# Router and output gates of a fused attention and mixture-of-experts kernel, moved from the vector engine to GpSimd under a new order of work

## The chip, the cores and the metric

The kernel runs on one core of one Trainium2 chip. The metric is device time in microseconds (us), the median of several runs. A run's time contains the span that the profile shows, from the first to the last instruction, and some microseconds around it. The engines are called by their names in the profile: PE multiplies matrices, PEld loads its weights, DVE is the vector engine, ACT the scalar engine, POOL is GpSimd, and SP only issues DMAs.

## The reference, cut to what matters

Two layers stand one after the other: attention over pooled keys and values for 8 heads, whose output is the input x of four causal attention experts, of which each token uses two.

```python
# q, k, v: (8 batches, 8 heads, 576 tokens, 64)
k_p = k.reshape(B, H, Sp, 8, D).mean(axis=3)          # 72 pooled keys
v_p = v.reshape(B, H, Sp, 8, D).mean(axis=3)
attn = softmax(scale * q @ k_p^T); x = (attn @ v_p)   # -> (8, 576, 512)

logits = x @ w_gate                                   # 4 experts
topk = the 2 largest; w = softmax over those two
for e in range(4):
    q, k, v = x @ wq[e], x @ wk[e], x @ wv[e]         # 512 -> 64
    a = softmax(causal(scale * q @ k^T))
    ye = a @ v @ wo[e]                                # 64 -> 512
    out += (e in topk) * w_e * ye
```

## The kernel before

The batches are worked on one after another, with two or three of them in flight at once. There are no loops over the work: line 551 begins a string, SEQ, of 1129 tokens, and lines 642 to 677 read it and issue each token's instructions. The order of the tokens is the order on PE, ACT, DVE and POOL; each engine takes its own tokens strictly in this order and waits for semaphores where data is not there. A token such as `P_q1:5@0c` names the step (P), its argument (q, pair of experts 1), the batch (5), the PSUM bank (0), and has a trailing d if a copy runs on DVE instead of ACT, or c if a matmul is cut into four strips of 32 columns of the PE array.

Capital letters are PE's steps. PK and PV pool keys and values (96x32 tiles of the array); KT, Q and T are transposes; E makes the first attention's scores and S the experts' scores (both use 64 rows of the array); D and O make the denominators and outputs of the first attention (96x32 tiles); P and V project to the experts' queries, keys and values (V also gives the router's logits, four columns wide); B multiplies with the values; Y is the output projection; H is a number of warm-up matmuls that compute nothing. The small letters read PSUM: kc, kt, vc, r, p, v, t and y copy results out (line 176, on ACT or DVE), e and s are exponentials on ACT (lines 267, 273, 427, 433), d and x make reciprocals by logarithm and exponential on ACT (lines 294, 298), o multiplies on DVE (lines 310, 317).

The steps that the change moves are these. `gate` (line 336), tokens g0 to g9 of each batch, turns logits L into weights G: g0 is an exponential on ACT (line 350), g1 to g4 find the second largest logit with pairs of maxima and minima and make a mask (lines 354, 359, 363, 367), g5 multiplies (371), g6 and g7 sum (373, 377), g8 takes a reciprocal (382), g9 multiplies (384). All but g0 are on DVE. `bv` (line 476) has three steps for each part of the experts' output: bz takes a reciprocal of the denominators from PSUM (482), bg multiplies it with G (484), b multiplies the output with that (489). All three are on DVE.

POOL issues every load (tokens L, line 117; L_q2:4 is the third sixth of the queries of batch 4; and W, line 130, for weights). A batch has 6 loads for q, 3 for k, 3 for v. POOL also zeroes the causal blocks after an exponential (token a, `am`, lines 442 and 450). Raw inputs have three buffers each, so a load of batch b waits until batch b-3 has been read. SP issues the output DMAs (lines 540 and 544); the token z, and the output's second half, go to ACT's queue.

Of the kernel before, what the change touches and what calls it, by code (L numbers as in the profile page):

```python
# [12 lines left out]
MINOP = mybir.AluOpType.min  # L13
MAXOP = mybir.AluOpType.max
ISGE = mybir.AluOpType.is_ge
ISLE = mybir.AluOpType.is_le
# [5 lines left out]
def kernel(  # L22
# [12 lines left out]
    nc = tc.nc  # L35
# [3 lines left out]
    E = moe_wq.shape[0]  # L39
# [296 lines left out]
    def gate(b, step):  # L336
# [10 lines left out]
        L = got("L")  # L347
# [3 lines left out]
        elif step == 1:  # L351
            L2 = L.rearrange("p c (a b) -> p c a b", b=2)
            for nm, op in (("hi", MAXOP), ("lo", MINOP)):
                nc.vector.tensor_tensor(
                    out=tmp(nm, 2, 1), in0=L2[:, :, :, 0:1], in1=L2[:, :, :, 1:2], op=op
                )
        elif step == 2:
            for nm, src, op in (("s2", "hi", MINOP), ("s3", "lo", MAXOP)):
                nc.vector.tensor_tensor(
                    out=tmp(nm, 1), in0=got(src)[:, :, 0, :], in1=got(src)[:, :, 1, :], op=op  # L360
                )
        elif step == 3:
            nc.vector.tensor_tensor(
                out=tmp("m2", 1), in0=got("s2"), in1=got("s3"), op=MAXOP
            )
        elif step == 4:
            nc.vector.tensor_tensor(
                out=tmp("msk", E), in0=L, in1=got("m2").to_broadcast([128, n, E]), op=ISGE
            )
        elif step == 5:  # L370
            nc.vector.tensor_mul(out=tmp("W", E), in0=got("Ex"), in1=got("msk"))
        elif step == 6:
            nc.vector.tensor_add(
                out=tmp("d2", 2), in0=got("W")[:, :, 0:2], in1=got("W")[:, :, 2:4]
            )
        elif step == 7:
            nc.vector.scalar_tensor_tensor(
                out=tmp("den", 1), in0=got("d2")[:, :, 0:1], scalar=1e-9,
                in1=got("d2")[:, :, 1:2], op0=ADD, op1=ADD,
            )  # L380
        elif step == 8:
            nc.vector.reciprocal(out=tmp("rden", 1), in_=got("den"))
        else:
            nc.vector.tensor_mul(
                out=tmp("G", E), in0=got("W"), in1=got("rden").to_broadcast([128, n, E])
            )
# [89 lines left out]
    def bv(b, bank, step, ep, part):  # L476
# [6 lines left out]
        elif step == "bg":  # L483
            nc.vector.tensor_mul(
# [26 lines left out]
    def Y(b, bank, c):  # L511
        p0 = 128 * place(b, c)
        last = (b, c) == (B - 1, 4)
        for n0 in (0, 256) if last else (0,):
            n = 256 if last else 512
            for ep in range(NEP):
                wide(psum[:, bank ^ (n0 > 0), n0 : n0 + n],
# [3 lines left out]
    def y(b, bank, dve, c, half=None, later=False):  # L521
        ofin = at[b, "ofin", c] if (b, "ofin", c) in at else ofp.tile([128, DM], FP32, name="ofin", tag="ofin")
        if half is not None:
            cols = slice(256 * half, 256 * half + 256)
            copy(half == 1, ofin[:, cols], psum[:, bank ^ half, cols])
# [10 lines left out]
    def z(b, c, queue):  # L536
# [15 lines left out]
        I:0 L_k0:0 L_k1:0 L_k2:0 J:0 K:0 H19:0@0 PK:0@0 kc:0 H4:0@1 KT:0@0 kt:0 L_q0:0 L_q1:0  # L552
        L_q2:0 L_q3:0 L_q4:0 L_q5:0 H8:0@1 Q2:0@0 r2:0 Q1:0@1 Q3:0@2 r1:0d r3:0 H1:0@3 E2:0@4
        e2:0 Q0:0@1 r0:0 E3:0@2 H5:0@0 E0:0@4 e3:0 L_v0:0 L_v1:0 E4:0@0 L_v2:0 PV:0@6 vc:0d e4:0
        e0:0 H2:0@2 D2:0@0 E1:0@2 O11:0@1 e1:0 H4:0@6 O01:0@2 O20:0@3 D1:0@4 d1:0 D0:0@5 x1:0
        M:0 L_k0:1 L_k1:1 L_k2:1 O10:0@6 O00:0@7 PK:1@4 d0:0 L_q0:1 o10:0 L_q1:1 L_q2:1 L_q3:1
        L_q4:1 kc:1d H3:0@5 KT:1@6 L_q5:1 H5:0@4 Q0:1@4 Q3:1@5 d2:0 x0:0 o01:0 o00:0 kt:1 o11:0
        x2:0 r0:1d W0:0 Q1:1@2 o20:0 W1:0 Q2:1@1 c0:0 E0:1@6 r3:1 r1:1d E3:1@4 c1:0d E1:1@2 e0:1
        c2:0d c3:0d P_q0:0@0 e3:1 W2:0 r2:1d W3:0 e1:1 P_t0:0@6 p_q0:0d p_t0:0d L_v0:1 P_k0:0@1
        S03:0@4 E4:1@6 E2:1@2 P_k1:0@0c c4:0d s03:0 L_v1:1 e4:1 V3:0@4c D2:1@5 D0:1@6 p_k1:0d  # L560
        p_k0:0d v3:0d P_q1:0@7c e2:1 D1:1@0 S00:0@2 d0:1 L_v2:1 d2:1 V1:0@6c p_q1:0d x0:1 s00:0
        V0:0@7c v0:0d PV:1@1 S01:0@2 S12:0@4 d1:1 V2:0@0c vc:1d x2:1 O20:1@1 v1:0d o20:1 s01:0
        O01:1@7 v2:0 L_k0:2 O11:1@6 x1:1 O00:1@2 L_k1:2 o01:1 o00:1 a03:0 O10:1@3 V4:1@0c o10:1
        o11:1 L_k2:2 s12:0 PK:2@1 P_t0:1@7 S02:0@4 kc:2 S10:0@2 g0:0 g1:0 v4:1 g2:0 KT:2@1
        L_q0:2 V3:1@6 V0:1@0 p_t0:1d s02:0 s10:0 g3:0 V2:1@7 kt:2d L_q1:2 L_q2:2 g4:0 L_q3:2
        L_q4:2 v3:1d L_q5:2 Q0:2@1 v2:1d Q3:2@6 v0:1 g5:0 r3:2d V1:1@2 Q1:2@0 Q2:2@3 r0:2 E0:2@6
        v1:1 E3:2@4 r1:2d a01:0 E1:2@0 e0:2 P_k0:1@2c g1:1 r2:2d P_q1:1@3c e1:2 g6:0 p_k0:1d
        e3:2 L_v0:2 L_v1:2 p_q1:1d D0:2@0 g0:1 L_v2:2 g7:0 g8:0 PV:2@1 vc:2d E2:2@6 d0:2 L_k0:3
        e2:2 E4:2@4 g2:1 P_q0:1@3c O00:2@2 L_k1:3 x0:2 O01:2@1 a00:0 O10:2@0 a10:0 L_k2:3 D1:2@6
        P_k1:1@7c e4:2 D2:2@4 d1:2 L_q0:3 x1:2 p_q0:1d d2:2 L_q1:3 a02:0 o01:2 O11:2@1 o00:2  # L570
        g3:1 PK:3@6 p_k1:1d L_q2:3 o11:2 S00:1@2 kc:3 S11:0@4 B01:0@7 L_q3:3 L_q4:3 o10:2 g4:1
        B00:0@6 g5:1 g6:1 g9:0 bz00:0 L_q5:3 KT:3@1 L_v0:3 P_q0:2@0 bz01:0 g7:1 kt:3d x2:2
        L_v1:3 g8:1 a12:0 g9:1 s11:0 L_v2:3 L_k0:4 p_q0:2d a11:0 V1:2@4 bg00:0 bg01:0 s00:1
        B10:0@5 v1:2 L_k1:4 S01:1@2 b00:0 S02:1@0 bz10:0 s01:1 L_k2:4 bg10:0 V0:2@4 L_q0:4
        L_q1:4 a01:1 B11:0@6 s02:1 b01:0 V3:2@7 Q1:3@2 v3:2 v0:2d Q2:3@4 b10:0 bz11:0 T0:0@5
        r1:3d S10:1@0 r2:3 bg11:0 E1:3@2 Q3:3@7 s10:1 b11:0 t0:0d r3:3d T1:0@6 Q0:3@5 P_k0:2@4
        S03:1@0 e1:3 t1:0d L_q2:4 L_q3:4 s03:1 L_q4:4 E3:3@6 r0:3d E4:3@2 e4:3 P_k1:2@5 L_q5:4
        p_k0:2d a00:1 p_k1:2d L_v0:4 E2:3@0 S12:1@2 PV:3@4 a03:1 e3:3 P_q1:2@5c vc:3d e2:3
        E0:3@0 s12:1 p_q1:2d W4:0 a02:1 L_v1:4 S11:1@6 B01:1@4 e0:3 bz01:1 bg01:1 B00:1@5 D1:3@2
        D2:3@3 O20:2@0 bz00:1 b01:1 o20:2 a12:1 s11:1 PK:4@1 D0:3@4 d1:3 d2:3 bg00:1 x1:3  # L580
        O00:3@6 L_v2:4 V2:2@0c O11:3@7 kc:4d O20:3@1 L_k0:5 b00:1 d0:3 o11:3 O10:3@3 v2:2 o10:3
        O01:3@2 Y3:0@5 a10:1 x0:3 P_t0:2@4 o01:3 Y1:0@0 x2:3 a11:1 o00:3 L_k1:5 B10:1@3 y3:0
        p_t0:2 Q0:4@2 y1:0 g1:2 o20:3 S01:2@4 S03:2@6 bz10:1 Y2:0@0c r0:4d s01:2 bg10:1 Y0:0@1c
        s03:2 PV:4@2 S02:2@4 b10:1 S12:2@6 y0:0d B11:1@3 g2:2 y2:0 vc:4d s02:2 Q1:4@0 Q2:4@1
        bz11:1 KT:4@2 Q3:4@4 T0:1@5 g3:2 r1:4d bg11:1 s12:2 kt:4d P_q0:3@0 b11:1 r3:4 r2:4d
        t0:1d E1:4@6 p_q0:3d e1:4 E3:4@2 E0:4@4 L_k2:5 P_k0:3@1 e3:4 T1:1@0 V2:3@6 P_q1:3@7
        E4:4@2 p_k0:3d g0:2 t1:1d g4:2 L_q0:5 L_q1:5 L_q2:5 v2:3d p_q1:3d e0:4 e4:4 S00:2@0
        E2:4@4 P_k1:3@6c e2:4 s00:2 Y3:1@7c L_q3:5 D0:4@2 L_q4:5 PK:5@3 D1:4@4 O11:4@5 y3:1d
        V1:3@7 p_k1:3d L_q5:5 d1:4 V0:3@0 Q3:5@4 kc:5 g5:2 L_v0:5 L_v1:5 v1:3d x1:4 KT:5@3 v0:3d
        Q0:5@7 P_t0:3@6 a12:2 Q1:5@0 r3:5d L_v2:5 d0:4 o11:4 r0:5d kt:5 Q2:5@1 S11:2@2 S10:2@4  # L590
        O00:4@7 p_t0:3 L_k0:6 x0:4 r1:5d O10:4@0 O01:4@6 L_k1:6 r2:5d s11:2 Y2:1@1c V4:3@2c
        o00:4 L_k2:6 L_q0:6 o01:4 s10:2 L_q1:6 a00:2 o10:4 D2:4@3 PV:5@7 Y0:1@6c y2:1 d2:4
        E4:5@4 vc:5 S00:3@0 L_q2:6 v4:3d y0:1d g6:2 a03:2 L_q3:6 L_q4:6 S02:3@2 x2:4 e4:5 V3:4@7
        g7:2 P_q0:4@6 L_q5:6 v3:4d s02:3 S10:3@4 p_q0:4d g8:2 s00:3 s10:3 S01:3@2 V3:3@7c L_v0:6
        v3:3d O20:4@6 P_k0:4@0c g1:3 o20:4 a11:2 s01:3 PK:6@1 p_k0:4d E1:5@4 g2:3 S11:3@6 e1:5
        E2:5@2 a01:2 a10:2 e2:5 P_k1:4@0 kc:6d g9:2 s11:3 B10:2@1 P_t0:4@4 Q3:6@5 V0:4@2 g3:3
        p_k1:4d L_v1:6 p_t0:4 bz10:2 L_v2:6 bg10:2 Y1:1@0 E3:5@6 a10:3 L_k0:7 g4:3 v0:4 r3:6d
        g0:3 E0:5@4 b10:2 y1:1 a02:2 S03:3@2 g5:3 B01:2@1 L_k1:7 B11:2@0 L_k2:7 s03:3 g6:3 a02:3
        B00:2@2 a00:3 g7:3 Q1:6@3 L_q0:7 e0:5 bz01:2 e3:5 KT:6@4 g8:3 g9:3 bz11:2 bg11:2 bg01:2
        V2:4@5 b11:2 L_q1:7 Q2:6@0 bz00:2 bg00:2 r1:6d b01:2 r2:6d D1:5@6 kt:6 D2:5@7 O10:5@4  # L600
        b00:2 a01:3 d1:5 d2:5 L_q2:7 v2:4d O01:5@3 x1:5 L_q3:7 x2:5 PV:6@1 D0:5@0 P_q1:4@7c
        O20:5@5 O00:5@2 vc:6d d0:5 a03:3 O11:5@6 x0:5 S12:3@0 o10:5 L_q4:7 T0:2@4 p_q1:4 a11:3
        o20:5 P_t0:5@5 o00:5 o01:5 s12:3 t0:2d p_t0:5 B01:3@7 B00:3@2 bz01:3 S02:4@0 o11:5
        L_q5:7 bg01:3 a12:3 bz00:3 s02:4 L_v0:7 E1:6@4 T1:2@3 B10:3@6 b01:3 V0:5@7 bg00:3 t1:2d
        bz10:3 V1:4@3 e1:6 bg10:3 v0:5 b00:3 S01:4@0 S00:4@4 b10:3 L_v1:7 Q0:6@2 v1:4d s01:4
# [99 lines left out]
```

The softmax here doesn't subtract the row's maximum and nothing guards it: scores larger than these inputs give would overflow.

## Time and profile before

| what | value |
|---|---|
| time, median of 3 runs | 167.99 us (167.83 to 222.52) |
| span of the profiled execution | 165.0 us |
| PE busy | 157.0 us, 95% (2463 matmuls, 51 of them warm-up) |
| ACT busy | 135.0 us, 82% (247 instructions) |
| DVE busy | 123.8 us, 75% (410 instructions) |
| POOL busy | 104.9 us, 64% (178 instructions) |
| last load issued | 102.8 us |

Busy time is the time in which an engine has an instruction of its own under way; PE's ends are modelled, so its share says little about how near it is to its peak. To see what it loses one reads the times at which matmuls start. Loads issued by POOL count as POOL's busy time[...]. A span of 165.0 us is the time from the first instruction to the last; the sums of the prediction are made against it.

### The profile page before, as it was taken

The numbers are of one execution on the slowest core, as the hardware profiler recorded it, in microseconds if no ns is written. First come the engines' busy times: TensorE is split into PE (matmuls) and PEld (weight loads), VectorE is DVE, ScalarE is ACT, GpSimd is POOL, SyncE is SP. The second block draws the span as 40 slices with busy tenths as digits, with TensorE's granted clock in tenths as the row PEclk, the third lists the DMA queues.
The fourth block names the chain that finished last, engine by engine and source line by source line (L and its number), as shares of the span: only waits on it lengthen the run. The fifth ranks groups of instructions, "written<-read, shape, count | busy, mean of one in ns | idle before, by whom it ended". The sixth has DMA issues, their size and how long they took to land. (4 is left out here: it accounts for less than half of the span.)

```text
span 165.0 us, 6106 instructions
## 1 busy us (share of the span) xinstructions
PE 157.0 (95%) x2463; PEld 93.8 (57%) x2463; DVE 123.8 (75%) x410; ACT 135.0 (82%) x247; POOL 104.9 (64%) x178
## 2 busy tenths in 40 slices
PE   6999988999999999999999999999999999999980
PEld 2344354568557656654754878555647686555730
DVE  1101497589799859976988899998998989779960
ACT  3029758999998999888998997789997999898860
POOL 6999891899999999965959997400140211364100
PEclk9999999999999999999999999999999999999998
DMA  2999999999999999999999999923113043055875
GB/s 22 160 153 171 164 172 178 170 145 139 177 156 173 164 157 148 156 233 217 206 178 226 168 198 83 174 100 86 47 68 127 4 131 127 0 190 195 257 260 191
DMA packets 84204, 25.04 MB, mean 152 GB/s; under 512 B 79312, under 2 KB 79568, under 8 KB 84176
## 3 DMA queue, kind: packets, MB, share of 16 engines
q0 software_dynamic: 78928, 15.21, 110.6%
q1 hardware_dynamic: 5024, 9.05, 15.9%
q8 instruction: 19, 0.31, 0.7%
q10 hardware_dynamic: 224, 0.39, 0.6%
q14 instruction: 9, 0.07, 0.1%
HBM read 30.42 MB, written 9.44 MB: 242 GB/s over the span
## 5 line engine op out<-in xcount | busy, mean ns | idle before, releaser
L433 ACT ACTIVATE etb_97<-psum 128x1024 bf16<-128x1024 f32 x24 | 23.6, 1023 | 2.5 <-PE psum L185 2.4
L433 ACT ACTIVATE etb_98<-psum 128x1024 bf16<-128x1024 f32 x24 | 23.5, 1027 | 1.3 <-PE psum L185 1.1
L450 POOL TENSOR_SCALAR_AFFINE_SELECT etb_98<-etb_98 128x256 bf16<-128x256 bf16 x32 | 12.5, 410 | 17.4 <-ACT etb_98 L433 17.2
L450 POOL TENSOR_SCALAR_AFFINE_SELECT etb_97<-etb_97 128x256 bf16<-128x256 bf16 x32 | 12.4, 415 | 15.8 <-ACT etb_97 L433 15.7
L173 PE MATMUL psum<-warm 128*128 128x512 bf16 x51 | 15.2, 443 | 1.8 <-DVE onesd L146 1.3
L273 ACT ACTIVATE eta_91<-psum 96x1024 bf16<-96x1024 f32 x16 | 15.9, 1018 | 1.1 <-PE psum L185 1.1
L273 ACT ACTIVATE eta_92<-psum 96x1024 bf16<-96x1024 f32 x16 | 15.6, 1020 | 0.7 <-PE psum L185 0.6
L117 POOL DMA_DIRECT2D qraw_68<-in_q_dram x18 | 13.9, 775 | 1.2 <-PE psum L185 1.1
L176 DVE COPY ofin<-psum 128x512 f32<-128x512 f32 (+1 forms) x18 | 11.9, 673 | 3.2 <-PE psum L185 2.4
L117 POOL DMA_DIRECT2D qraw_69<-in_q_dram x18 | 13.8, 770 | 0.5 <-issue 0.5
L176 DVE CAST qk_99<-psum 128x512 bf16<-128x512 f32 (+1 forms) x16 | 10.5, 670 | 3.8 <-PE psum L185 3.6
L176 DVE CAST qk_100<-psum 128x512 bf16<-128x512 f32 (+1 forms) x16 | 10.5, 654 | 3.5 <-PE psum L185 3.5
L176 ACT COPY ofin<-psum 128x512 f32<-128x512 f32 (+1 forms) x19 | 10.7, 580 | 2.7 <-PE psum L185 1.8
L185 PE MATMUL psum<-wvg,xT_96 128*32 128x260 bf16 (+1 forms) x120 | 10.8, 275 | 0.0
L173 PEld LDWEIGHTS <-warm 128*128 128x128 bf16 x51 | 5.1, 111 | 9.5 <-issue 5.8
L185 PE MATMUL psum<-wvg,xT_95 128*32 128x260 bf16 (+1 forms) x156 | 10.5, 275 | 0.0
L185 PEld LDWEIGHTS <-etb_97 128*128 128x128 bf16 x240 | 8.8, 97 | 2.0 <-issue 0.4
L117 POOL DMA_DIRECT2D qraw_70<-in_q_dram x12 | 9.2, 784 | 0.0
L185 PEld LDWEIGHTS <-etb_98 128*128 128x128 bf16 x240 | 8.3, 97 | 1.4 <-issue 0.8
L185 PE MATMUL psum<-qk_100 64*128 64x64 bf16 (+4 forms) x96 | 8.8, 276 | 0.1
L117 POOL DMA_DIRECT2D kraw_71<-in_k_dram x9 | 7.0, 787 | 2.7 <-DMA qraw_70<-in_q_dram 1.8
L185 PE MATMUL psum<-qk_99 64*128 64x64 bf16 (+4 forms) x96 | 8.4, 277 | 0.0
(198 smaller groups left out, 452.8 us busy)
## 6 DMA issues: line engine op xcount, KB each, us to landing
out_dram<-ofin SPq DMA_DIRECT2D x31, 256.0 KB, 3.0
kraw_71<-in_k_dram POOLq DMA_DIRECT2D x9, 192.0 KB, 6.2
qraw_68<-in_q_dram POOLq DMA_DIRECT2D x18, 96.0 KB, 5.3
vraw_74<-in_v_dram POOLq DMA_DIRECT2D x9, 192.0 KB, 5.5
kraw_72<-in_k_dram POOLq DMA_DIRECT2D x9, 192.0 KB, 5.9
qraw_69<-in_q_dram POOLq DMA_DIRECT2D x18, 96.0 KB, 5.5
vraw_75<-in_v_dram POOLq DMA_DIRECT2D x9, 192.0 KB, 4.9
kraw_73<-in_k_dram POOLq DMA_DIRECT2D x6, 192.0 KB, 6.5
```

The source lines that it names most:

```text
L117: nc.gpsimd.dma_start(out=dst, in_=src)
L173: nc.tensor.matmul(out=psum[:, bank, :], lhsT=warm[:, 0:128], rhs=warm[:], start=True, stop=True)
L176: (nc.vector.tensor_copy if dve else nc.scalar.copy)(out=out, in_=in_)
L185: nc.tensor.matmul(out=out, lhsT=lhsT, rhs=rhs, start=start, stop=stop)
L273: nc.scalar.activation(out=eta[:, hp, :, 0:MAIN], in_=psum[0:KR, bank : bank + 2, :], func=EXP, scale=ATT_EXP_SCALE,)
L433: nc.scalar.activation(out=et[:, ep, :, eo : eo + n], in_=psum[:, bank : bank + 2, 0:n], func=EXP, scale=MOE_EXP_SCALE,)
L450: nc.gpsimd.affine_select(out=blk, in_=blk, pattern=[[0, 2], [1, 128]], compare_op=ISGE, fill=0.0, base=0, channel_multiplier=-1,)
```

## The change

The gate's steps g1 to g6 and g9 move from DVE to POOL. The mask is made in another way: instead of finding the second largest logit, all 4x4 differences of logits are made (g1), compared with zero (g2), and summed (g3, g4), which gives each expert's number of larger logits; the mask is where it is below two (g5). g7 and g8 stay on DVE, g0 on ACT. The step bg of the output gates moves from DVE to POOL; bz and b stay on DVE. The last output block uses bank and bank + 1 in place of bank and bank ^ 1. The whole string SEQ is replaced: the same steps in another order, on other banks, with other copies on DVE, other matmuls cut in strips (50 in place of 34), 46 warm-up matmuls in place of 51, and no z token.

```diff
         elif step == 1:
-            L2 = L.rearrange("p c (a b) -> p c a b", b=2)
-            for nm, op in (("hi", MAXOP), ("lo", MINOP)):
-                nc.vector.tensor_tensor(
-                    out=tmp(nm, 2, 1), in0=L2[:, :, :, 0:1], in1=L2[:, :, :, 1:2], op=op
-                )
+            nc.gpsimd.tensor_sub(
+                out=tmp("Df", E, E), in0=L.unsqueeze(3).to_broadcast([128, n, E, E]),
+                in1=L.unsqueeze(2).to_broadcast([128, n, E, E]),
+            )
         elif step == 2:
...
+            nc.gpsimd.tensor_scalar(out=got("Df"), in0=got("Df"), scalar1=0.0, scalar2=None, op0=ISLT)
         elif step == 3:
...
+            nc.gpsimd.tensor_add(
+                out=got("Df")[:, :, :, 0:2], in0=got("Df")[:, :, :, 0:2], in1=got("Df")[:, :, :, 2:4]
+            )
         elif step == 4:
...
+            nc.gpsimd.tensor_add(
+                out=got("Df")[:, :, :, 0], in0=got("Df")[:, :, :, 0], in1=got("Df")[:, :, :, 1]
+            )
         elif step == 5:
-            nc.vector.tensor_mul(out=tmp("W", E), in0=got("Ex"), in1=got("msk"))
+            nc.gpsimd.tensor_scalar(
+                out=tmp("msk", E), in0=got("Df")[:, :, :, 0], scalar1=2.0, scalar2=None, op0=ISLT
+            )
+            nc.gpsimd.tensor_mul(out=tmp("W", E), in0=got("Ex"), in1=got("msk"))
         elif step == 6:
-            nc.vector.tensor_add(
+            nc.gpsimd.tensor_add(
...
         else:
-            nc.vector.tensor_mul(
+            nc.gpsimd.tensor_mul(
                 out=tmp("G", E), in0=got("W"), in1=got("rden").to_broadcast([128, n, E])
             )
...
         elif step == "bg":
-            nc.vector.tensor_mul(
+            nc.gpsimd.tensor_mul(
...
-                wide(psum[:, bank ^ (n0 > 0), n0 : n0 + n],
+                wide(psum[:, bank + (n0 > 0), n0 : n0 + n],
...
     SEQ = """
-        I:0 L_k0:0 L_k1:0 L_k2:0 J:0 K:0 H19:0@0 PK:0@0 kc:0 H4:0@1 KT:0@0 kt:0 L_q0:0 L_q1:0
-        L_q2:0 L_q3:0 L_q4:0 L_q5:0 H8:0@1 Q2:0@0 r2:0 Q1:0@1 Q3:0@2 r1:0d r3:0 H1:0@3 E2:0@4
...
-        bz02:7 Y2:7@1 bg02:7 bg12:7 y3:7 b02:7 y2:7p Y0:7@0 z2:7 y0:7 Y1:7@2 b12:7 T12:7@4
-        t12:7d y1:7 t12:6d T02:7@6 t02:7d Y4:7@6 ya4:7 yb4:7d
+        I:0 L_k0:0 L_k1:0 J:0 L_k2:0 K:0 H14:0@7 PK:0@6 kc:0d H5:0@7 KT:0@0 kt:0d L_q0:0 L_q4:0
+        L_q2:0 L_q3:0 L_q5:0 L_q1:0 L_v1:0 L_v2:0 L_v0:0 L_k1:1 L_k2:1 H9:0@7 Q1:0@1 L_k0:1 L_q4:1
...
+        P_k0:1@0 E0:2@6 a12:0 e2:2 e1:2 r3:2d E3:2@1 e3:2 g1:0 P_q0:1@3c L_k0:4 g2:0 e0:2 L_v0:3
+        g3:0 g4:0 p_k0:1d PV:2@0 S01:0@4 D1:2@1 vc:2d P_k1:1@2c p_q0:1d s01:0 g5:0 g6:0 d1:2 p_k1:1d
...
+        s00:3 Q2:5@6 T0:1@7 KT:5@3 r0:5d V3:3@5 r2:5d t0:1d Q1:5@0 r1:5d kt:5 Q3:5@4 r3:5d v3:3
+        L_q2:6 E0:5@1 e0:5 S11:2@6 L_k0:7 D2:4@5 O11:4@0 Y3:1@3c Y2:1@4c o11:4 y2:1d L_q2:7 d2:4
...
+        T01:7@2 Y1:7@1 B02:7@0 bz12:7 b11:7 bg12:7 bz02:7 T11:7@5 y1:7 Y0:7@4 t01:7d t11:7 Y2:7@5
+        y0:7 bg02:7 b02:7 T02:7@0 t02:7 b12:7 T12:7@1 y2:7d Y3:7@4 t12:7 y3:7 Y4:7@0 ya4:7 yb4:7d
     """
```

In the new order the loads of a batch stand further down among the other steps of POOL: 53 of the 100 operations that POOL gains come before the last load.

## The prediction

> **What bounds the kernel now.** The profiled execution spans 165.0 us, the median of the runs is 167.99 us: 3.0 us lie around the span. I read the busy time by stretches first (columns: stretch, its length, PE, PEld, DVE, ACT, POOL busy with instruction counts, TensorE clock, DMA share, GB/s).
> ```profile
> 26.00:56.00 30.00, 29.95 (x547) 19.05 (x544) 24.78 (x81) 27.75 (x55) 26.29 (x40) 1.00 1.89 162
> 56.00:86.00 30.00, 30.00 (x514) 17.71 (x511) 24.15 (x66) 27.99 (x53) 24.59 (x40) 1.00 1.79 183
> 86.00:116.00 30.00, 29.92 (x543) 19.24 (x542) 26.92 (x86) 26.76 (x50) 18.46 (x34) 1.00 1.27 152
> 116.00:146.00 30.00, 30.00 (x486) 19.11 (x484) 26.21 (x89) 27.04 (x47) 7.97 (x21) 1.00 0.22 77
> ```
> PE is always busy, but its ends are modelled, so I next read start-to-start times in the timeline of PE.
> ```profile
> 31.57 0.39 PE L185 MATMUL psum<-eta_92,onesd 96*32 96x512 bf16 x4
> 31.89 0.39 PE L185 MATMUL psum<-qk_99 64*128 64x512 bf16 x2
> ...
> 57.45 1.04 PE L185 MATMUL psum<-xT_96,wkp_123 128*128 128x512 bf16 x4
> 58.42 0.42 PE L185 MATMUL psum<-qT_89,kpT_80 64*96 64x512 bf16 x2
> ```
> A warm 512-column pass takes 0.216 us to the next one of its kind (most common spacing in the trace); four 32-column matmuls, or two of 64 rows, share one pass. So four full passes should take 0.86 us and take 0.97 (57.45 to 58.42); one shared pass should take 0.22 and takes 0.32. The extra **0.11 us is paid each time the tile shape changes**. Mean over all changes: 0.115.
>
> From the first projection (26.2 us) to the last matmul (160.6 us) are 134.4 us. The matmul counts by shape times their own spacings (0.216 per 512-column pass, 0.110 per 260 columns, 0.042 per 96-column transpose, 0.029 per 64 or 65 columns) make 121.2 us; the order has 80 changes of shape there, 9.2 us. That leaves **4.0 us of true waiting**: PE bounds the kernel. The view of its waits names only 1.4 us after 26 us:
> ```profile
> PE psum L185 <- ACT qT_90 L176: 0.7, 1, 0.7
> PE psum L185 <- DVE oT_111 L176: 0.4, 1, 0.4
> PE psum L185 <- DVE ofin L176: 0.3, 1, 0.3
> ```
> Ahead of 26.2 us PE waits for loads and fills with warm-up matmuls. Last, POOL's own timeline and groups:
> ```profile
> 65.55 4.57 POOL L117 DMA_DIRECT2D qraw_70<-in_q_dram  x6
> ...
> 119.10 1.13 POOL L450 TENSOR_SCALAR_AFFINE_SELECT etb_97<-etb_97 128x256 bf16<-128x256 bf16 x3 [8.60 <-ACT etb_97 L433]
> ```
> ```profile
> L689 POOL MEMSET const-float32-1.0<- 128x1 f32 x1 | 0.1, 98 | 0.0
> L484 DVE TENSOR_TENSOR gt_105<-rzb_103,G 128x4 f32<-128x4 f32 (+2 forms) x18 | 3.2, 182 | 0.2
> ```
> A load holds POOL 0.77 us, a mask 0.36 us to the next. From 26 to 86 us POOL is 85% busy, nearly all of it with the loads that feed PE later.
>
> **What the skill says.** (1) The Trainium skill, TensorEngine Tiling (Array Packing), Key Properties: changing the tiling mode drains TensorE. The trace agrees: 0.11 us. (2) The Trainium skill, GPSIMD Engine Reference, 3.1: a two-input elementwise operation costs about 2.6 cycles an element at 1.2 GHz, plus dispatch in software. The trace before has no two-input POOL operation. (3) The Trainium skill, SBUF — State Buffer, Who interferes with whom: DVE and GpSimd share a port pair as an exclusive lock. The trace shows no POOL stall that I can put down to it; the change leaves fewer two-input DVE operations, so I cost it at 0 (bounds 0 and +1 us).
>
> **The change part by part.**
>
> *Off DVE.* Per batch nine gate operations (hi, lo, two of L359, L363, L367, L371, L373, L384) and in all 36 of L484. By their rows: 1.7+1.5+2.6+1.4+1.4+1.4+1.4+1.4 = 12.8 us, and 6.4 us: 19.2 us off. Copies planned anew (DVE's share before to after): y 17 to 21, p 32 to 33, r 24 to 27, kc 3 to 8, kt 3 to 5, vc 7 to 5, t 21 to 13. At DVE's 0.69, 0.69, 0.45, 0.68, 0.4, 0.68 and some 0.35 us this gives back 4.8 us: DVE falls by some 14 us. ACT changes by -4x0.59 -0.60 -3x0.65 -5x0.58 -2x0.48 +2x0.58 +8x0.4 = -4.4 us. Neither engine ends the chain; they can return at most PE's 4.0 us of waits. About 1 us of it lies in the last ten us, where DVE is 9.4 of 10 busy. I take -1.3 (bounds -4.0 and 0).
>
> *PE.* The same passes. Warm-up goes from 51 to 46; all but one lie ahead of the first projection: cost 0, the cover is the wait for the batch-1 loads (23.0 us) and the weights (24.5 us on), which stand behind 21 loads in both orders. Fewer copies on ACT there may start the first projection earlier: -0.4 (0 to -1). Changes of shape from that point go from 80 to 93, counted in the order (E and S are 64-row; PK, PV, D, O and every token with a c are 32-column; the rest full): 13 x 0.115 = **+1.5** (bounds +1.4 and +2.9, where a change out of 32-column tiles would cost 0.22).
>
> *Onto POOL.* 8 operations a batch (g1, g2, g3, g4, two of g5, g6, g9) and 36 bg: **100 operations**. Price: lower bound 0.10 (the MEMSET row), upper 0.45 (above the mask's 0.41 duration for 256 elements). Estimate from (2): 64 elements 0.14 us, 16 elements 0.03, plus 0.10 of the MEMSET and the 0.07 that POOL needs after a release (end of the exp to start of its mask, in the trace): 0.31 to 0.18, mean 0.22. All are chained, so I hide none behind the next.
>
> These stand between the loads. Ahead of the last q load of batch 6 the new order has 83 loads, 5 weight loads, 20 masks and 25 gate operations: 83x0.769 + 5x0.85 + 20x0.36 + 0.25 (iota) = 75.5, +25x0.22 = 81.0, +1.4 (POOL's start) = 82.4 us, +6 us of landing (medians 5.3 to 6.0 for q; up to 9 where loads run densely) = 88.4 us. PE would want it at 26.2 + 54.7 us of passes + 48 changes x 0.115 = 86.4 us: **2.0 us late**. The same sum gives 1.6 late for batch 4, 0.3 for batch 5, 1.1 early for batch 7. In the order before, it gives 2 to 17 us early, which is why PE does not wait for loads there. Late loads don't add up (a PE that waited wants the next one later): 2.0, plus 1.0 for what POOL itself waits in its queue, which delays every load behind it: **+3.0** (at 0.10 an operation and 5 us landing: 0; at 0.45 and 6 us: 7.7, plus waits 9).
>
> *The added hop.* DVE's bz, POOL's bg, DVE's b: two hand-overs of 0.07 where DVE needed 0.03, so some 0.15 us each with the slower operation; behind a load it waits up to 0.77 us. DVE's strict order queues the next copies behind b, and PE needs their banks. 36 x 0.15 = 5.4 us, nearly all beside PE since DVE has 14 us more room; I take +1.0 (0 to +4).
>
> *Banks, and the last output.* The halves of the last Y go to bank and bank+1: 0. SP now issues the row block that ACT's queue issued (0.33 to 0.6 us each): 0 to +0.5, taken as 0.
>
> Sum: -1.3 -0.4 +1.5 +3.0 +1.0 = +3.8: a span of 168.8, a time of **171.8 us**.
>
> **The rivals.** *POOL stays hidden* (0.40). POOL's operations are cheap enough that batch 6 comes in time; what is left is +1.5 for the shapes, +0.8 for hops, -1.7 for DVE and ACT: 168.6 us. For it: 98 ns of a MEMSET, and the skill's price is mostly a fixed part that may overlap. Against: the chain is serial. The point from which it decides: batch 6's 25 operations must fit in 86.4 - 1.4 - 75.5 - 6 = 3.5 us, 0.14 each, or 0.18 each if a load lands in 5 us. *PE loses all its waits* (0.10): ACT, 89 to 93% busy, and DVE are what PE's 4.0 us come from; the shapes cost +1.5 and the head gives 1: 168.0 - 4.0 - 1.0 + 1.5 = 164.5 us. Against it: ACT loses only 3% of its work. *Slower by more*, inside my forecast's half: 0.45 an operation gives 168 + 9 + 1.5 + 1 - 1.7 = 177.8. That the change doesn't do what it says: not possible for the moved operations; for the plan, the passes are the same by count.
>
> **How the numbers follow.** Forecast 0.50 (slower by over 2%, above 171.35), hidden POOL 0.40 (within 2%, which is about what a measurement of this kernel can tell from no change), waits gone 0.10 (faster, under 164.63). The predicted 171.8 is the likeliest case's. The range 165.5 to 178.0 leaves out most of the third case and what lies past the 0.45 price: some 0.2 together. The forecast's own range is 171.4 to 178.
>
> **What would show it.** Right: PE idle before qraw of batches 4 to 6, released by a DMA, some 2 to 4 us in all between 60 and 95 us; POOL near 125 us of busy time, full to about 100 us; DVE near 110; ACT near 130. Wrong: no load wait on PE (the price is under 0.14 to 0.18), or PE waits on DVE copies that stood behind b (the hop is dearer), or a shape change cheaper than 0.1.

## The result and the profile after

The changed kernel takes 174.69 us in the median (174.15 to 177.61, 5 runs), the kernel before 167.83 us beside it: a ratio of 1.044, with a 95% interval of 1.039 to 1.049. It is slower, as forecast, and 2.9 us slower than the predicted 171.8. Here and below, ratios and their intervals leave out executions over 1.5% above the fastest of the same kernel, while medians count them all.

The one profile taken with these runs has TensorE at half its clock from 17.1 to 27.4 us, so all readings below are from a second profiled execution of the same kernel (174.7 us, span 172.7 us), in which the clock is full from 5 to 169 us. First the busy time in the same stretches as before (columns: stretch, length, PE, PEld, DVE, ACT, POOL busy with instruction counts, TensorE clock, DMA share, GB/s).
```profile
26.00:56.00 30.00, 26.60 (x579) 14.37 (x575) 20.56 (x50) 24.32 (x45) 26.18 (x43) 1.00 1.88 162
56.00:86.00 30.00, 29.41 (x583) 19.60 (x582) 21.78 (x59) 27.17 (x49) 29.38 (x59) 1.00 1.57 133
86.00:116.00 30.00, 29.30 (x611) 16.60 (x612) 24.04 (x58) 27.49 (x48) 24.04 (x60) 1.00 1.31 175
116.00:146.00 30.00, 30.00 (x612) 19.64 (x601) 23.45 (x61) 26.92 (x53) 14.25 (x47) 1.00 0.26 58
```
PE now has holes, stretches in which no matmul is under way, most of them in the first stretch, 3.4 us of 30. DVE is clearly relieved (20.6 against 24.8), and POOL went from 24.6 to 29.4 of 30 in the second stretch: it is full. The view of PE's waits (engine, line, what it waited for; us in total, times, longest), for the same kernel:
```profile
PE psum L184 <- DVE L L175: 2.7, 1, 2.7
...
PE psum L184 <- issue: 1.3, 2, 0.7
...
PE psum L184 <- DVE xT L309: 0.6, 1, 0.6
PE psum L193 <- DMA qraw<-in_q_dram: 0.5, 1, 0.5
```
The load wait of the last line lies at the head of the kernel; between 26 and 100 us no matmul waits for a load. The largest hole ends in a DVE copy. PE's, DVE's and POOL's timelines around it (start, duration, instruction; in brackets the idle time ahead of it and what ended that):
```profile
48.08 0.40 PE L184 MATMUL psum<-eta,vp 96*32 96x512 bf16 x4
51.14 1.05 PE L184 MATMUL psum<-xT,wqp 128*32 128x512 bf16 x16 [2.66 <-DVE L L175]
```
```profile
47.43 0.15 DVE L175 COPY L<-psum 128x4 f32<-128x4 f32 x1
50.52 0.16 DVE L375 SCALAR_TENSOR_TENSOR den<-d 128x4 f32<-128x4 f32 x1 [2.93 <-POOL d L371]
50.60 0.43 DVE L175 CAST vaug<-psum 128x256 bf16<-128x256 f32 x1
50.94 0.15 DVE L175 COPY L<-psum 128x4 f32<-128x4 f32 x1
```
```profile
46.76 0.30 POOL L351 TENSOR_TENSOR Df<-L 128x64 f32<-128x64 f32 x1
47.00 0.81 POOL L116 DMA_DIRECT2D kraw<-in_k_dram  x1
47.83 0.40 POOL L356 TENSOR_SCALAR Df<-Df 128x64 f32<-128x64 f32 x1
48.16 0.82 POOL L116 DMA_DIRECT2D vraw<-in_v_dram  x1
49.01 0.25 POOL L358 TENSOR_TENSOR Df<-Df 128x32 f32<-128x32 f32 x1
...
50.28 0.20 POOL L371 TENSOR_TENSOR d<-W 128x8 f32<-128x8 f32 x1
```
Read upward from PE: the query projection of batch 1 needs the bank that V3 of batch 1 has filled. The copy that empties it (50.60 on DVE) stands behind `den`, step g7 of batch 0's gate. `den` waits 2.93 us for `d`, POOL's last step of that gate, and POOL's chain is late because two loads of 0.8 us stand inside it, and loads fill POOL's queue ahead of it from 35 us on.

To compare kernels I use the prediction's own sum for each profile: the first projection's start, the passes, the changes of tile shape at 0.115 us, what is left up to the last four matmuls (waits, and what any stretch at a lower clock adds), and the time from these four on. "Waits" is the remainder, so each row closes whatever the other terms are worth. All in us.

| kernel | first projection | passes | shapes | waits | end | span |
|---|---|---|---|---|---|---|
| before | 26.2 | 120.7 | 9.2 | 3.9 | 5.0 | 165.0 |
| changed | 26.4 | 120.9 | 10.7 | 8.1 | 6.6 | 172.7 |

The waits by their place, as the excess of a step's start-to-start time over its passes and its shape change: 2.85 at 48 us (the chain above), 0.97 at 61 us (the same chain for batch 1), 0.90 at 37 us and 1.08 at 99 us (inside projections cut in strips, no releaser shown), 2.3 for all else.

### The profile page after: what moved, and what is told of

Read it like the earlier page. It is cut to its first block, busy times and chain, and to the rows that moved or that the text cites. A ratio compares the mean times of both kernels' runs of the same rounds, so it can differ in the third digit from the quotient of the medians.

```text
span 175.6 us, 6784 instructions
## 1 busy us (share of the span) xinstructions
PE 161.3 (92%) x2806; PEld 95.2 (54%) x2824; DVE 115.6 (66%) x307; ACT 133.0 (76%) x242; POOL 127.9 (73%) x278
## 4 chain that ended last, share of the span: by engine, by line
PE 85%; POOL 5%; DMA 4%; issue 2%; DVE 0%; POOLq 0%; ACT 0%; DVEq 0%; ACTq 0%
PE psum L184 72%; PE psum L193 9%; DMA vraw<-in_v_dram 4%; PE psum L172 4%; POOL qraw L116 3%; POOL kraw L116 1%; POOL vraw L116 1%; DVE ofin L175 0%; POOL diff L149 0%; POOLq L149 0%; ACT oT L175 0%; DVEq L175 0%; ACTq L175 0%; POOLq L683 0%
## 5 line engine op out<-in xcount | busy, mean ns | idle before, releaser
L431 ACT ACTIVATE etb<-psum 128x1024 bf16<-128x1024 f32 x48 | 48.0, 1025 | 3.7 <-PE psum L184 3.4
L116 POOL DMA_DIRECT2D qraw<-in_q_dram x48 | 37.4, 783 | 4.5 <-DMA vraw<-in_v_dram 1.9
L272 ACT ACTIVATE eta<-psum 96x1024 bf16<-96x1024 f32 x32 | 31.4, 1020 | 3.2 <-PE psum L184 3.0
L448 POOL TENSOR_SCALAR_AFFINE_SELECT etb<-etb 128x256 bf16<-128x256 bf16 x64 | 24.7, 405 | 3.2 <-ACT etb L431 3.1
L175 DVE CAST qk<-psum 128x512 bf16<-128x512 f32 (+1 forms) x33 | 21.0, 644 | 5.7 <-PE psum L184 5.2
L184 PE MATMUL psum<-wvg,xT 128*32 128x260 bf16 (+1 forms) x336 | 23.3, 287 | 0.2 <-issue 0.2
L316 DVE TENSOR_TENSOR xT<-psum,rza 128x512 bf16<-128x512 f32 x32 | 21.3, 682 | 2.1 <-PE psum L184 1.9
L184 PE MATMUL psum<-xT,wkp 128*32 128x64 bf16 (+3 forms) x352 | 19.9, 284 | 2.3 <-issue 2.1
L184 PE MATMUL psum<-xT,wqp 128*32 128x64 bf16 (+3 forms) x365 | 19.7, 286 | 0.4 <-issue 0.2
L482 POOL TENSOR_TENSOR gt<-rzb,G 128x4 f32<-128x4 f32 (+2 forms) x36 | 7.0, 202 | 17.1 <-DVE rzb L480 11.2
L184 PE MATMUL psum<-vaug,etb 128*128 128x65 bf16 x480 | 19.1, 193 | 0.2
L487 DVE TENSOR_TENSOR osc<-psum,gt 128x256 bf16<-128x256 f32 (+2 forms) x36 | 15.5, 441 | 3.0 <-POOL gt L482 2.8
L175 DVE COPY qT<-psum 128x576 bf16<-128x576 bf16 x27 | 11.5, 451 | 5.1 <-PE psum L193 4.3
```

The source lines that it names most:

```text
L116: nc.gpsimd.dma_start(out=dst, in_=src)
L175: (nc.vector.tensor_copy if dve else nc.scalar.copy)(out=out, in_=in_)
L184: nc.tensor.matmul(out=out, lhsT=lhsT, rhs=rhs, start=start, stop=stop)
L272: nc.scalar.activation(out=eta[:, hp, :, 0:MAIN], in_=psum[0:KR, bank : bank + 2, :], func=EXP, scale=ATT_EXP_SCALE,)
L316: nc.vector.tensor_tensor(out=xT[:, 2 * g + t, mcols(b)], in0=psum[:, bank, :], in1=rz[:, g, 0:MAIN], op=MULT)
L431: nc.scalar.activation(out=et[:, ep, :, eo : eo + n], in_=psum[:, bank : bank + 2, 0:n], func=EXP, scale=MOE_EXP_SCALE,)
```

## The experiments

I began with two theories. **A**: the loss is TensorE's own (its clock, its instructions' supply for the many short strips, the shapes, the head of the kernel). **B**: it comes from GpSimd's queue and the added hop, as predicted. The first profile, with its low clock and a hole of 2 us at 42 us inside a cut projection, spoke for A. Later expectations call the sharpened forms S (supply and order on TensorE) and Q (GpSimd's queue).

**The changed kernel again.**

> The changed kernel once more, for a second profile. Theory A (matmul engine: its clock, its instruction supply and its shape changes) expects some 174.5 us, a stall of about 2 us near 42 us in the middle of the 64-column projection of batch 1, cut in strips, named as issue and not as a semaphore, and a first projection no later than 30.7 us; where the clock stays full ahead of 28 us, a first projection 2 to 3 us earlier than that. Theory B (POOL's queue delays loads and output gates, as the prediction had it) expects waits of the matmul engine for q loads of batches 4 to 6, 2 to 4 us in all, between 60 and 95 us.

Measured: 174.51 us, ratio 1.041 (1.035 to 1.047), the profiled execution at full clock up to 169 us. The low clock in the head is no part of the median's loss: with it absent the time is the same (the execution that had it took 177.61 us). A's hole inside the cut projection is there, at 37 us, but with 0.90 us and not 2. B's waits for q loads between 60 and 95 us are not there at all.

**Projections whole again.** The four 64-column projections P_t0 of batches 0, 1, 2 and 4 lose their c:
```diff
-L_q2:3 P_t0:1@2c p_t0:1 V4:1@6c
+L_q2:3 P_t0:1@2 p_t0:1 V4:1@6c
```


> The changed kernel with the four 64-column projections (batches 0, 1, 2 and 4) no longer cut in strips: 16 matmuls and 16 weight loads each in place of 64 and 64. Theory A expects the 2 us stall near 42 us and the half clock that follows it to go: 2.5 to 4 us faster than the changed kernel, 170.5 to 172 us, though up to four more shape changes at 0.115 us. Theory B expects no change (174 to 175 us), since POOL's queue is the same.

Measured: 174.94 us, ratio 1.044 (1.038 to 1.050). No gain, as B said. But its profile shows no hole at 37 or 99 us any more, which is 2.0 us saved (that at 99 us stood in a projection of 512 columns, which keeps its strips). The one at 48 us grew from 2.85 to 3.61 us: POOL's chain ends when it ends, and PE merely arrives earlier to wait for it. That takes back 0.8 us. The uncut projections bring seven more changes of shape, 0.8 us by the price. And right after the longer hole TensorE runs at half clock, from 52.2 to 55.6 us, where PE loses some 1.4 us more than in the profile above.

**Warm-up moved in the head.**
```diff
-PV:0@2 vc:0d
+H6:0@7 PV:0@2 vc:0d
...
-H8:0@7 Q0:1@3
+H4:0@7 Q0:1@3
```


> The changed kernel with six more warm-up matmuls ahead of the first pooling of values and four fewer ahead of the transposes of batch 1. Theory A expects the clock to stay full ahead of 28 us and the first projection to start 2 to 4 us earlier than 30.7 us; 1 to 4 us faster than the changed kernel, 170.5 to 173.5 us. Theory B expects no change (174 to 175 us).

Measured: 174.56 us, ratio 1.039 (1.032 to 1.046). No gain; the first projection starts at 26.4 us, against 26.4 in the changed kernel and 26.2 before. A's account of the head is out.

**All gates back on VectorE**, in the form of the kernel before, under the new order:
```diff
-            nc.gpsimd.tensor_mul(
+            nc.vector.tensor_mul(
                 out=gt[:, :, :, 0], in0=rz[:, :, :, 0],
```


> The changed kernel's order, banks and copies, but the router gates computed as before (maxima and minima) and all gate operations back on the vector engine. Theory B expects the loads and hand-overs to be in time again: 3 to 4 us faster, 170.5 to 171.5 us. Theory A expects no gain: POOL is not on the path, and the vector engine gets 19 us back, so 174 to 177 us.

Measured: 177.82 us (177.52 without one of 180.62), ratio 1.057 (1.047 to 1.066). B in its plain form misses, and A's 174 to 177 is nearer: the move of the gates is worth some 3 us to this order. The hole at 48 us is gone (waits in steps that begin between 40 and 50 us fall from 2.96 to 0.13), but new ones come late, 1.8 and 0.9 us from 153 us on, where DVE stands at a gate step whose logits come from ACT; a spell at half clock follows, from 156.5 to 159.9 us. The order is planned for gates that are not on DVE.

**Loads behind the gates.** Five loads inside the gates' chains of batches 0 and 1 go behind them:
```diff
-g1:0 P_q0:1@3c L_k0:4 g2:0 e0:2 L_v0:3 g3:0
+g1:0 P_q0:1@3c g2:0 e0:2 g3:0
...
-g5:0 g6:0 d1:2
+g5:0 g6:0 L_k0:4 L_v0:3 d1:2
...
-a11:0 g6:1 g7:1
+a11:0 g6:1 L_q4:4 L_q2:4 L_q3:5 g7:1
```


> The changed kernel with one edit in GpSimd's order: five loads that stood between the router's small ops (two in batch 0's chain, three in batch 1's) are put behind the last of them. Theory Q (gates wait behind loads in GpSimd's in-order queue, VectorE waits behind them at its den step, and TensorE behind VectorE for a bank): VectorE's wait for d falls from 4.8 us to about 2.5, TensorE's 2.7 us wait before the first query projection of batch 1 (near 48 us) falls to about 1 and the 0.6 one near 61 us goes, so some 2 to 2.5 us off: about 172.2. Theory S (the loss lies in TensorE's own order and its instruction supply; a wait removed here is met again a little later): 174 to 175, no change.

Measured: 175.13 us, ratio 1.045 (1.038 to 1.052). The total of Q is missed, its places are not: the hole at 48 us falls from 2.85 to 1.28 us, the one at 61 us is gone. A new one of 2.27 us stands at 64 us, and its lines name the same queue. POOL, DVE and PE there:
```profile
65.82 0.21 POOL L482 TENSOR_TENSOR gt<-rzb,G 128x6 f32<-128x6 f32 x1
```
```profile
66.06 0.56 DVE L487 TENSOR_TENSOR osc<-psum,gt 128x384 bf16<-128x384 f32 x1 [2.89 <-POOL gt L482]
```
```profile
66.67 0.40 PE L184 MATMUL psum<-eta,onesd 96*32 96x512 bf16 x4 [2.14 <-DVE osc L487]
```
The loads that were moved stand ahead of the first output gate, gt, in both orders, so POOL comes to it no sooner: at 65.8 us here, at 64.7 in the changed kernel. PE, which no longer waits at 48 and 61 us, is there earlier and waits now. In this full queue the reordering moved the wait to the next customer. In this profile TensorE then runs at half clock from 67.9 to 71.3 us, which takes another 0.7 us in one projection.

**Both edits.**

> The same edit, and the four 64-column projections that the change cut into 32-row strips are whole again (192 matmuls fewer on TensorE, three shape changes more). Done alone, this second edit gave nothing because the wait at 48 us took up what it saved. Theory Q: with the wait shortened the saving shows, some 0.9 us at 37 us and perhaps another 1 us near 99 us, against 0.35 us for the shape changes: about 171 to 171.5. Theory S: the strips are a loss by themselves, so 173 to 173.5 here too, but then the earlier run with only this edit should have shown it and did not.

Measured: 176.78 us, ratio 1.053 (1.048 to 1.058), a miss and slower than either edit. This kernel has a fifth projection whole, that of batch 5 (P_t0:5), which the expectation does not count: 240 matmuls fewer and nine changes of shape more, 1.0 us and not 0.35. The profile, of an execution of 178.11 us, has 2.18 us at 48 us, 2.26 at 64 us, and half clock from 67.2 to 74.0 us. Why the whole comes out slower than the sum of its parts is not settled.

**The move alone, in the old order.** Before's order, banks and copies, with the gates on POOL:

> The kernel before with its own order, banks and copy engines, and only the move: the router's gates and the output gates run on GpSimd as in the change. Theory Q: its order was made for gates on VectorE and has many loads between the gate steps, so the gates come late and VectorE, then TensorE, wait: 170 to 174. Theory S (the move itself is harmless or helps, and the new order costs): 166.5 to 168.

Measured: 193.4 us in the median, 189.25 in the fastest of four: at least 21.9 us slower than before, and far outside Q's own figure. Here the wait that the prediction was about appears: POOL stands at a gate's first step for its logits, with loads behind it. The profile is of an execution of 193.47 us, with 13.7 us at half clock in three spells before the end. POOL, then PE:
```profile
36.36 0.29 POOL L351 TENSOR_TENSOR Df<-L 128x64 f32<-128x64 f32 x1 [5.05 <-DVE xT L309]
36.74 0.37 POOL L356 TENSOR_SCALAR Df<-Df 128x64 f32<-128x64 f32 x1
37.08 0.84 POOL L116 DMA_DIRECT2D qraw<-in_q_dram  x1
```
```profile
41.51 0.22 PE L193 MATMUL psum<-ident,qraw 96*128 96x96 bf16 x1 [1.08 <-DMA qraw<-in_q_dram]
42.42 0.22 PE L193 MATMUL psum<-ident,qraw 96*128 96x96 bf16 x1 [0.70 <-DMA qraw<-in_q_dram]
```
The two halves of the change do not add up: the move in the old order makes 189 us or more, the new order without the move 177.5 ("All gates back on VectorE"), both together 174.5, and neither 167.3.

**The output gates alone, in the old order** (the one line of the diff above, the other way):

> The kernel before with only the output gates (36 small multiplies) on GpSimd. The prediction's term for this hop was +1.0 us, so 168.8; if the loads in GpSimd's queue stand ahead of these multiplies too (theory Q), more, 169 to 172, with waits of VectorE for gt; theory S: within 0.5 us of before.

Measured: 172.81 us (172.58 without one of 175.3), ratio 1.031 (1.028 to 1.034), just above Q's range: 36 multiplies of 0.2 us cost some 5.3 us. The largest part that its profile names is in what stands behind them. POOL stands 1.42 us at one of them at 68.7 us and 2.51 at the next; the q loads of batch 6 come behind it, from 82.6 to 87.3 us where the kernel before issues them from 78.7 to 84.4. PE then reads the queries of batch 6 one load at a time from 94.5 us on, each late. POOL, then PE:
```profile
71.43 0.20 POOL L484 TENSOR_TENSOR gt<-rzb,G 128x4 f32<-128x4 f32 x1 [2.51 <-DVE m L363]
```
```profile
94.54 0.22 PE L194 MATMUL psum<-ident,qraw 96*128 96x96 bf16 x1 [0.44 <-DMA qraw<-in_q_dram]
95.17 0.22 PE L194 MATMUL psum<-ident,qraw 96*128 96x96 bf16 x1 [0.41 <-DMA qraw<-in_q_dram]
```
**The first two gates back on VectorE.** In the changed kernel, batches 0 and 1 take the old gate, all else stays on POOL:
```diff
     def gate(b, step):
+        if b < 2:
+            return gate_v(b, step)   # steps g0 to g9 as before the change
```


> The changed kernel with the router's gates of batches 0 and 1 back on VectorE in the form of the kernel before, at the same places of the order; the later batches' gates and all output gates stay on GpSimd. GpSimd was busy for 97 to 99% of the stretch from 50 to 90 us, and 16 of its small ops go from 46 to 65 us. Theory Q (between 35 and 90 us GpSimd is the bound, and the waits of 2.9 us at 48 us and 1.0 us at 60 us are its backlog reaching TensorE): both waits go, and no new one of over 1 us comes before 90 us, 171.5 to 172.3. Rival P (the planned order needs every gate off VectorE, which is why all gates back on VectorE was slower): 174.5 to 177, with VectorE late in that stretch.

Measured: 172.19 us (171.43 without one of 176.88), ratio 1.027 (1.020 to 1.035); the profiled execution spans 169.6. The holes at 48 and 61 us are both gone, and the largest other between 40 and 160 us is 0.7 us, at 56 us, where PE waits for a copy that stands behind the gate's steps on DVE. As Q says, at the edge of its figure; P is out. The hole at 37 us, inside P_t0:1, has grown from 0.90 to 1.72 us: PE comes to it 0.5 us earlier and goes on 0.3 us later.

**With the projections whole (those of batches 0, 1, 2, 4 and also 5) and the last output on SyncE's queue:**
```diff
-(nc.scalar if h and b == B - 1 else queue).dma_start(
+queue.dma_start(
```


> The same, the four 64-column projections whole, and the last 128 KB of the output on SyncE's queue and not on ScalarE's. Theory Q: with no wait on GpSimd left to take up what the projections save, 0.9 us at 37 us and some 1 us near 99 us show, less 0.35 for the shape changes, and the end after the last matmul shrinks from 6.3 us by 0.5 to 1: about 169.5 to 170.5. Rival P: 173 to 176. If e8 is right and this stays at e8's time, the strips' instruction supply is no cost of its own.

Measured: 168.96 us, ratio 1.011 (1.007 to 1.014), 0.5 us below Q's range. The edit that gave nothing alone now shows: the waits fall from 5.8 to 3.0 us, of which nine changes of shape more take back 1.0. PE at P_t0:1 with strips (the kernel of the last experiment) and without (this one):
```profile
37.03 0.23 PE L186 MATMUL psum<-xT,wkp 128*32 128x64 bf16 x4
38.69 0.39 PE L186 MATMUL psum<-xT,wkp 128*32 128x64 bf16 x28 [1.43 <-issue]
```
```profile
37.05 0.41 PE L186 MATMUL psum<-xT,wqp 128*128 128x64 bf16 x8
37.29 0.40 PE L186 MATMUL psum<-xT,wkp 128*128 128x64 bf16 x8
37.62 1.08 PE L186 MATMUL psum<-wvg,xT 128*32 128x260 bf16 x32
```
The time from the last four matmuls on falls by 0.7 us, from 6.64 to 5.95.

**The output gates alone back on VectorE**, the router's gates staying on POOL:

> The changed kernel with only the 36 output multiplies back on VectorE; the router's gates stay on GpSimd. GpSimd loses 7 us of work and some 17 us of standing at these multiplies for VectorE. Theory Q with the output gates as a main cause (as in the kernel before, where moving them alone cost 5.5 us): 171 to 173. Rival: in the new order they hurt nothing, and going back loads VectorE as all gates back did: 175 to 177; then the router's gates are what the planned order gained from or lost by.

Measured: 176.93 us, ratio 1.059 (1.056 to 1.063). The rival's figure is right: in the new order nothing is gained by taking the output gates off POOL, and the kernel is about 2.4 us slower for it. The 2.4 us at 48 us stay. How much of the loss is DVE's load is not shown: of the 1.8 us by which this profile's waits exceed the changed kernel's, some 1.5 lie in a spell at half clock right after that hole, from 50.7 to 54.1 us, which the changed kernel's second profile does not have.

**The strips alone, in the old order.** P_t0 of batches 0, 1, 2 and 4 get a c in the kernel before:

> The kernel before with one thing of the change alone: the 64-column projections of batches 0, 1, 2 and 4 cut into 32-row strips (192 matmuls and weight loads more, each short; five shape changes more, 0.6 us by the price of 0.115). Theory S as it stands now (such strips use up TensorE's instructions faster than 16 KB fetches[...] bring them): inside at least one cut projection TensorE stands with no releaser for 0.4 to 1.7 us, most likely batch 1's near 37 us, and the time is 168.5 to 170. Rival: the waits in the changed kernel came from the place of its fetches, not from the strips; no such wait here, 167.5 to 168.2.

Measured: 170.08 us, ratio 1.019 (1.014 to 1.023). Slower as S says, by 2.9 us, with an interval on both sides of 2%, though the holes without a releaser are short, 0.3 to 0.4 us, the first in the strips of a V that follows and the second in P_t0:1:
```profile
33.78 0.97 PE L185 MATMUL psum<-wvg,xT 128*32 128x260 bf16 x28 [0.38 <-issue]
38.61 0.30 PE L185 MATMUL psum<-xT,wqp 128*32 128x64 bf16 x16 [0.34 <-issue]
```
Of the 2.4 us that this execution's span is longer, 0.6 are the five shape changes, 1.2 waits, and 0.65 the first projection's start, which lies ahead of most strips and which I can't put down to them. So the strips cost about 1.8 us here, 0.6 of it by a price that was counted and not measured.

The other sums follow. "Waits" is the remainder here too: the 28.9 of "before, gates on POOL" hold what 13.7 us at half clock add, and a spell of 3.4 us at half clock stands in each of the first four rows.

| kernel | first projection | passes | shapes | waits | end | span |
|---|---|---|---|---|---|---|
| changed, projections whole | 25.7 | 120.9 | 11.5 | 8.4 | 6.5 | 173.0 |
| all gates on DVE | 25.8 | 120.9 | 10.7 | 12.1 | 6.3 | 175.7 |
| loads behind gates | 26.0 | 120.9 | 10.7 | 10.1 | 6.4 | 174.0 |
| output gates on DVE | 25.6 | 120.9 | 10.7 | 9.9 | 6.5 | 173.7 |
| first two gates on DVE | 25.6 | 120.9 | 10.7 | 5.8 | 6.6 | 169.6 |
| the same, whole, last output on SP | 25.9 | 120.9 | 11.7 | 3.0 | 6.0 | 167.5 |
| before, gates on POOL | 27.1 | 120.7 | 9.2 | 28.9 | 5.9 | 191.8 |
| before, output gates on POOL | 26.1 | 120.7 | 9.2 | 9.7 | 5.7 | 171.3 |
| before, strips | 26.9 | 120.7 | 9.8 | 5.1 | 5.0 | 167.4 |

The best mixture still stays 1% behind the kernel before: it waits 0.9 us less than that, and gives back 2.5 us for 22 more shape changes and 1.0 us at the end. No version here beats the kernel before.

## Why the prediction was right, and where its terms were not

The verdict and the resource were right, GpSimd's queue shared by loads and gates. The way it reaches TensorE was not the one priced. Term by term, against the span of 172.7 (7.7 above before; 3.8 were forecast):

- *Relief of DVE and ACT, -1.3*: the waits other than the four named ones fell from 3.9 to 2.3 us, so -1.6. The size is right; that the relief made it is not shown apart. DVE is busy 115 us (110 expected): the durations of its instructions sum to 15.5 us less, near the 14 forecast, but they overlap, and busy time falls by 8.8 only. ACT is busy 133 (130 expected).
- *Head, -0.4*: the first projection starts at 26.4 against 26.2 us, +0.1.
- *Shapes, +1.5*: 93 changes, as counted. Their price was not tested: no run changed the shapes alone.
- *Late loads, +3.0*: this step failed; it came to 0. No load of batches 4 to 6 was late. The price of an operation was nearly right by duration, 0.24 us in the mean (24.0 us for 100) against 0.22, but not as a chain: with no load between them, seven of a gate hold POOL 2.35 us (47.61 to 49.96 us in "Loads behind the gates"), 0.34 each. The sum's other parts were off and cancelled: POOL issues batch 6's last q load at 87.9 us, some 5 us later than summed, most of it because POOL stood 4.6 us ahead of loads between 16 and 45 us (mostly until an earlier load had landed), where 1.0 was allowed; PE, itself late, wants it at 92.5, 6 us later than summed; and the load lands in 4.5 us and not 6, 0.1 us ahead of its reader. In the mixture that ends at 167.5 us it is 0.7 us ahead. The mechanism is real, but in the old order (the two experiments with gates moved there), whose loads stand behind gates that wait.
- *In its place, +3.8*: the same queue the other way round. Gates wait behind loads, DVE waits at g7 behind them, PE behind DVE: 2.85 us at 48 and 0.97 us at 61 us. Taking just those two batches' gates off POOL removed both. The prediction had looked for what is queued behind a waiting POOL instruction; it priced the hop bz to b, and did not ask the same of DVE's g7 behind POOL's g6.
- *The hop, +1.0*: not found at those steps in the new order, where DVE waits 3.0 us in all for gt, no wait of PE ends there, and taking the hop back made the kernel 2.4 us slower; in the old order it is some 5.3.
- *Not in the sum, +2.0*: the waits inside strips, 0.90 and 1.08 us, which the prediction put at nothing. I counted strips as shape changes only, and not as four times the instructions.
- *Banks and last output, 0 (to +0.5)*: +1.6. The issue of the last 128 KB takes 2.07 us on ACT's queue where it took 0.54, with an instruction fetch of 8 KB under way at 167.5; moving it to SP's queue gave back 0.6 to 0.7. The rest of the end's growth is not settled.

With +0.2 for the passes these make -1.6 +0.1 +1.5 +3.8 +2.0 +1.6 +0.2 = 7.6.

That the verdict came out right is in part luck: the term that carried it measured 0, and 7.4 us that the sum did not have or put at nothing (gates behind loads, strips, the end) stood in its place. By this sum the changed kernel without these would be within 2% of the one before.

Of the rivals, the hidden POOL had the right observation (no load wait) and the wrong reason and conclusion: an operation took 0.24 us and not under 0.18. *What would show it* listed the miss, "PE waits on DVE copies that stood behind b": they stood behind g7.

## What to carry to other kernels

When work moves into a queue that also issues the loads, price both directions: the loads behind it, and the engine that waits for its result, with everything queued behind that wait. In this queue, 97 to 99% full from 50 to 90 us, reordering moved the wait and taking work out removed it: five loads moved gave nothing, 16 small operations taken off cut PE's waits by 2.3 us. And a saving that lies upstream of the longest wait can show as nothing until that wait is gone, so an edit that measures zero should be tried again after it.

## What the runs showed of the hardware

- The mask's small operations on GpSimd cost mainly a fixed part: two-input operations took 0.22 us for 16 elements and 0.30 us for 64, compare-with-scalar ones 0.26 and 0.39. The Trainium skill, GPSIMD Engine Reference, 3.1, puts the per-element cost of two inputs at about 2.6 cycles; the slope here, 0.076 us for 48 elements, is 1.6 ns or 1.9 cycles at the 1.2 GHz given there, less than the page has, and the measurement decides. The fixed part of about 0.2 us is what counts. Chained without a load between them (49.01 to 50.28 us in the lines above) such operations start 0.30 to 0.33 us apart.
- TensorE can stand with nothing that the profile names to wait for. Strips make many short instructions: in the profile of the changed kernel read above 32 matmuls of 64 columns, each with its weight load, start from 37.22 to 37.55 us, and after four more it stands. The profiles show 13 such holes of 0.2 to 2.0 us inside strips (of 64, 260 and 512 columns), and each ended 2.2 to 3.0 us after a transfer of 16 KB of instructions had begun: the 1.43 us up to 38.69 us with one begun at 36.45, the 1.98 us up to 44.06 in the first profile with one begun at 41.84. With the 64-column projections whole there was none at 37 us. That the transfer is the cause is inferred from this lag; no run changed the transfers alone.
- Near the end of a hole of about 2 us or more TensorE often fell to half clock for 3.4 or 6.8 us. Outside the kernel with all gates moved in the old order, seven of these profiles show it (from 44.4, 50.7, 50.9, 52.2, 67.2, 67.9 and 156.5 us on), from 0.5 us before to 1.3 us after the hole's end. It did not after 2.85 us at 48 us in the changed kernel's second profile, nor after 2.18 us at 48 us with both edits. Where such a spell follows the hole at 48 us, PE loses 1.2 to 1.6 us more by 57 us than where none follows: a hole can cost more than its length.
- The Trainium skill, Perfetto Trace Analysis, DMA Optimizations, advises to balance transfers over the engines that can issue them where descriptor generation is the bottleneck. This trace has that picture, a load holding GpSimd for 0.77 us and GpSimd busy 23.8 of the 24 us from 66 to 90; moving loads off it was not tried.
